# Attention features on one core: Omega loaded without its zeros, two transposes and K products moved behind a later pair's first products, half the k/q loads in another buffer ring

## The chip, the cores and the metric

The kernel runs on one core of a Trainium2 chip. The metric is the device time of one execution in microseconds (us). A core has five engines with instruction streams of their own: PE (TensorE, matrix products), DVE (VectorE), ACT (ScalarE), POOL (GpSimd) and SP (SyncE, which here only issues DMA transfers). Each stream runs in its order; where it needs another engine's result it waits on a semaphore.

## The reference

Random-feature attention, then two feed-forward layers. What the change touches is the first part, for 2 x 8 heads of 576 tokens with 64 channels and 128 features:

```python
scale = 1.0 / np.sqrt(np.sqrt(D))
q_s, k_s = (q * scale, k * scale)
def phi(x):
    proj = np.einsum('bhsd,md->bhsm', x, omega)
    h = proj - np.sum(x * x, axis=-1, keepdims=True) / 2.0
    h = h - np.max(h, axis=-1, keepdims=True)
    return np.exp(h) / np.sqrt(m)
kv = np.einsum('bhsm,bhsd->bhmd', phi(k_s), v)
z = np.sum(phi(k_s), axis=2)
out = einsum(phi(q_s), kv) / (einsum(phi(q_s), z) + 1e-06)
```

Then `x = (h * tanh(softplus(h))) @ w_out` with `h = x @ w_in` for 1152 tokens, a gate over 8 experts, and one expert of 512 x 1024 x 512 for each token. The change leaves those two layers as they are.

## The kernel before

**Pairs and steps.** Heads go in eight pairs, p = 0 to 7. A pair's tile `kqf` has the two heads' channels on 128 partitions, and its columns are groups of 128 tokens of k or q. Omega stands in a block-diagonal tile of 128 x 256 (`omf`, with `oms`, `omh`, `oml` made from it), so one product gives both heads' features. A pair is worked off in steps t = 0 to 3 (and 4, the tokens 512 to 575 of two pairs, for odd pairs), written here as (p,t). `proj(p, t)` makes a 128 x 512 result `pj`, by two times three products: L72 high part by high part, L73 high part of k/q by low part of Omega, L74 low part by high part. Only (0,0) is one plain fp32 product (L248), because it can start before k and q are split into their parts `kqh` and `kql`.

**After each step.** `phi(p, t)`: DVE takes the negated maximum (`nm`, L259), for odd t DVE also subtracts it for the q half (L264), then ACT writes exp of the k half (L266) into the tile `e`, and for even t the shifted q half as well (L269). `kvm` multiplies e of k by v into one bank, `kvp` (L278), and `qtr` transposes the q half on PE into `qt` (L299). Both are done one pair later: pair 0's at pair 1's steps.

**Result banks.** Results `pj` rotate over three banks, but some steps share a tile of two banks, `twin`:

```python
if (p, t) in ((0, 3), (1, 3)):
    st["twin"] = twin("pj")
first = {(0, 3): 0, (1, 0): 1, (1, 3): 0, (1, 4): 1}
```

So (0,3) and (1,0) lie in the two halves of one tile, and (1,3) and (1,4) in the halves of the next. The order of instructions on each engine comes from a list scheduler; `issue_after` adds a constraint to it.

**Splitting.** Pair 0 is split by ACT (L56) and DVE (L63), pair 1 by POOL (L58, L63) and partly DVE (L60), all others by POOL.

**Loads.** SP issues them all in one order, apart from Omega's (ACT, L189). All pairs' `kqf` share two buffers, `v` has three. The ring `raw` of four buffers of 128 x 512 int64 (as many bytes as 128 x 1024 fp32) takes `w_in` and `w_out` from L136.

Of the kernel before, what the change touches and what calls it, by code (L numbers as in the profile page):

```python
# [9 lines left out]
F32 = mybir.dt.float32  # L10
# [3 lines left out]
I64 = mybir.dt.int64  # L14
U32 = mybir.dt.uint32
AF = mybir.ActivationFunctionType
ALU = mybir.AluOpType
AX = mybir.AxisListType

NB, NH, SEQ, HD, M = 2, 8, 576, 64, 128  # L20
# [8 lines left out]
SCALE = 1.0 / math.sqrt(math.sqrt(HD))  # L29
# [4 lines left out]
def performer_mish_moe(  # L34
# [44 lines left out]
    ident = cs[:, 0:128]  # L79
# [51 lines left out]
    win, wo, raw = {}, {}, {}  # L131
# [53 lines left out]

    with ExitStack() as c2:
        a1 = c2.enter_context(tc.tile_pool(name="a1", bufs=1))
        omf = a1.tile([128, 2 * M], F32, name="omf")
        nc.scalar.dma_start(out=omf, in_=omt)  # L189
        omh = a1.tile([128, 2 * M], F32R, name="omh")  # L190
        oml = a1.tile([128, 2 * M], F32R, name="oml")
        a2 = c2.enter_context(tc.tile_pool(name="a2", bufs=2))
# [3 lines left out]
        wp = twin("wp")[:, 1, :]  # L196
        for _ in range(5):
            T.matmul(out=wp, lhsT=nc.const_aps.tensor(1.0, [128, 128], BF16), rhs=nc.const_aps.tensor(1.0, [128, 512], BF16), start=True, stop=True)
        oms = a1.tile([128, 2 * M], F32, name="oms")
        V.tensor_scalar(out=oms, in0=omf, scalar1=SCALE, scalar2=None, op0=ALU.mult)  # L200
        V.tensor_scalar(out=omh, in0=omf, scalar1=SCALE, scalar2=None, op0=ALU.mult)
        V.scalar_tensor_tensor(out=oml, in0=omf, scalar=SCALE, in1=omh.bitcast(F32), op0=ALU.mult, op1=ALU.subtract)
        st = {}


# [3 lines left out]
            return [slice(*c) for c in zip(cuts, cuts[1:])]  # L209

        def load(p):
            f = a3.tile([128, 1280], F32, name="kqf", tag="kqf", bufs=2)
            v = a3.tile([128, 780], F32, name="v", tag="v")
            for c in pieces(p):
                nc.sync.dma_start(out=f[:, c], in_=kq[p][:, c])
            st[p] = dict(f=f, v=v, e={})
            if p % 2 == 0:
                st[p // 2, "u"] = {}
# [18 lines left out]
        def proj(p, t):  # L237
            d = st[p]
# [4 lines that stand above are left out]
            d["p", t] = ps = st["twin"][:, first[p, t], :] if (p, t) in first else bank("pj", "pj")  # L243
            for i in range(2):
                s = slice(256 * t + 128 * i, 256 * t + 128 * i + 128)
                if (p, t) == (0, 0):

                    T.matmul(out=ps[:, i * 256 : i * 256 + 256], lhsT=d["f"][:, s], rhs=oms, start=True, stop=True)  # L248
                    continue
                with tc.issue_after(d["mm"].ins) if p == 0 and (t, i) > (1, 0) else ExitStack():  # L250
                    d["mm"] = mm3(ps[:, i * 256 : i * 256 + 256], d["h"][:, s], d["l"][:, s], omh, oml, True, True)

        def phi(p, t):

# [16 lines left out]
        def kvm(p, h):  # L271

            d, du = st[p], st[p // 2, "u"]
            if p % 2 == 0 and h == 0:
                du["K"] = bank("b0", "kvp")
            e, v, K, c = d["e"], d["v"], du["K"], (2 * h + p % 2) * 65
            for t in range(4):
                T.matmul(out=K[:, c : c + 65], lhsT=e[t][:, h, :], rhs=v[:, (2 * t + h) * 65 : (2 * t + h + 1) * 65], start=(p % 2 == 0 and h == 0 and t == 0), stop=False)  # L278
            if p % 2:
                T.matmul(out=K[:, h * 130 : h * 130 + 130], lhsT=e[4][:, h, :], rhs=v[:, 520 + h * 130 : 650 + h * 130], start=False, stop=(h == 1))  # L280

# [9 lines left out]
        def qtr(p, h):  # L291
            e, d = st[p]["e"], st[p // 2, "u"]
            if p % 2 == 0 and h == 0:
                d["qT"] = a2.tile([128, 2, 2, SEQ], F32, name="qT", tag="qT")
            qT = d["qT"]
            q = bank("qt", "qt")
            if h < 2:
                for t in range(4):
                    T.transpose(q[:, t * 128 : t * 128 + 128], e[t][:, 2 + h, :], ident)  # L299
                S.activation(out=qT[:, p % 2, h, 0:512], in_=q, func=AF.Exp)  # L300
            else:
                for i in range(2):
                    T.transpose(q[:, i * 128 : i * 128 + 128], e[4][:, 2 + i, :], ident)
                S.activation(out=qT[:, :, :, 512:SEQ], in_=q[:, 0:256].rearrange("p (h r t) -> p r h t", h=2, r=2), func=AF.Exp)
# [703 lines left out]
def _layout(a):  # L1008
    import numpy as np

    q, k, v, om = a["q"], a["k"], a["v"], a["omega"]
    kq = np.zeros((NPAIR, 128, 1280), np.float32)
    va = np.zeros((NPAIR, 128, 780), np.float32)
    for p in range(NPAIR):
        b, hp = divmod(p, NPAIR // NB)
        c = p % 2
        vm = va[p, :, 0:520].reshape(128, 4, 2, 65)
        vt = va[p - p % 2 + 1, 64 * c : 64 * c + 64, 520:780].reshape(64, 2, 2, 65)
        vm[..., 64] = 1.0
        vt[:, :, c, 64] = 1.0  # L1020
        for h in range(2):
            r = slice(64 * h, 64 * h + 64)
            for i, x in ((0, k), (1, q)):
                x = x[b, 2 * hp + h].T
                kq[p, r, 0:1024].reshape(64, 4, 2, 128)[:, :, i] = x[:, 0:512].reshape(64, 4, 128)
                kq[p - c + 1, r, 1024 + 128 * i + 64 * c : 1088 + 128 * i + 64 * c] = x[:, 512:]
            x = v[b, 2 * hp + h]
            vm[:, :, h, 0:64] = x[0:512].reshape(4, 128, 64).transpose(1, 0, 2)
            vt[:, h, c, 0:64] = x[512:]
    omt = np.zeros((128, 2, M), np.float32)  # L1030
    omt[0:64, 0] = om.T
    omt[64:128, 1] = om.T
    wi = np.ascontiguousarray(a["moe_w_in"].view(np.int64).reshape(2, 4, 2, 32, NJ, 128).transpose(4, 1, 3, 0, 2, 5)).reshape(NJ, 128, 512)
    wo = np.ascontiguousarray(a["moe_w_out"].view(np.int64).reshape(NJ, 128, 512))
    wg = np.zeros((4, 32, DM // 32, 4, E), np.float32)
    for i in range(4):
        wg[i, :, :, i] = a["moe2_w_gate"].reshape(DM // 32, 32, E).transpose(1, 0, 2)
    cst = np.zeros((128, 352), np.float32)
    cst[:, 0:128] = np.eye(128)
    cst[:, 128:224] = np.tile(np.arange(E) - 1000, NTT)  # L1040
    cst[0:TT, 224:320] = np.triu(np.ones((TT, TT)), 1)
    cst[:, 320:352] = np.tile(np.eye(32), (4, 1))
    return dict(
        kq=kq,
        va=va,
        omt=omt.reshape(128, 2 * M),
        w_in=wi,
        w_out=wo,
        wgate=wg.reshape(128, DM // 32, 32),
        w1=np.ascontiguousarray(a["moe2_w1"]),  # L1050
        w2=np.ascontiguousarray(a["moe2_w2"]),
        cap=np.asarray(a["moe2_capacity"]).astype(np.int64).reshape(1, 1),
        cst=cst,
    )
# [16 lines left out]
```

## Time and profile before

| | |
|---|---|
| median of 3 runs | 298.11 us (297.5 to 298.68) |
| the profiled execution's own time | 298.33 us |
| its span, from the first to the last instruction | 296.5 us |
| PE busy | 288.7 us, 97% of the span |
| DVE, ACT, POOL busy | 214.6, 188.1, 72.9 us |
| of the chain that ended last | PE 94%, DMA 3% |

The profile is of one execution. 1.83 us of its time lie around the span. A matmul's duration includes its pipeline, so rows overlap; the pace is read from the distance of two starts.

### The profile page before, as it was taken

How to read it: one execution, taken by the hardware profiler on the slowest of the kernel's cores; microseconds unless marked ns; L12 is line 12 of the kernel's file. 1: busy time of each engine (PE TensorE's matmuls, PEld its weight loads, DVE VectorE, ACT ScalarE, POOL GpSimd, SP SyncE). 2: the span in 40 equal slices, each digit the busy share in tenths (PEclk: the TensorE clock that was granted, in tenths of full speed). 3: DMA queues.
4: the chain of work that ended last, by engine and by line, in shares of the span. 5: the costliest groups of instructions: out<-in, count | busy, mean ns of one | idle time of the engine just before them, and what ended most of it. 6: DMA issues, size and time to landing. Idle time of an engine off the chain costs nothing.

```text
span 296.5 us, 6008 instructions
## 1 busy us (share of the span) xinstructions
PE 288.7 (97%) x2276; PEld 269.6 (91%) x2277; DVE 214.6 (72%) x394; ACT 188.1 (63%) x370; POOL 72.9 (25%) x108
## 2 busy tenths in 40 slices
PE   8999999999999999999999999999999999999992
PEld 5898888877999999999979988889999999999991
DVE  4675757996999999899897199958557674437420
ACT  4787787875194787978957989444446465245211
POOL 2798996233021101010111276200000000000000
PEclk9999999999999999999999999999999999999997
DMA  7955831221266479945610000000445528702011
GB/s 247 301 183 180 284 119 54 73 78 66 70 212 212 154 220 320 342 144 150 221 58 0 0 2 0 3 0 3 140 123 165 144 65 270 204 32 82 0 42 45
DMA packets 18433, 37.09 MB, mean 125 GB/s; under 512 B 1632, under 2 KB 7616, under 8 KB 18400
## 3 DMA queue, kind: packets, MB, share of 16 engines
q1 hardware_dynamic: 18256, 36.53, 38.8%
q8 instruction: 19, 0.31, 0.4%
q10 hardware_dynamic: 144, 0.13, 0.2%
q14 instruction: 14, 0.11, 0.2%
HBM read 33.12 MB, written 3.54 MB: 124 GB/s over the span
## 4 chain that ended last, share of the span: by engine, by line
PE 94%; DMA 3%; POOL 0%; DVE 0%; issue 0%; ACT 0%
PE h L72 12%; PE h L74 11%; PE h L73 11%; PE py L72 9%; PE py L74 9%; PE py L73 9%; PE kvp L278 4%; PE ph L74 3%; PE ph L72 3%; PE ph L73 3%; PE pj L72 3%; PE num L311 3%; PE lg L503 3%; PE pj L74 3%; PE pj L73 2%; PE qt L299 2%
## 5 line engine op out<-in xcount | busy, mean ns | idle before, releaser
L72 PE MATMUL h<-xh,wih 128*128 128x384 f32 x192 | 64.7, 337 | 0.0
L74 PE MATMUL h<-xh,wil 128*128 128x384 f32 x192 | 64.3, 335 | 0.0
L73 PE MATMUL h<-xl,wih 128*128 128x384 f32 x192 | 64.2, 334 | 0.0
L72 PE MATMUL py<-gh,whi 128*128 128x288 f32 x128 | 38.4, 300 | 0.0
L74 PE MATMUL py<-gh,wl 128*128 128x288 f32 x128 | 37.7, 295 | 0.0
L73 PE MATMUL py<-gh,whi 128*128 128x288 f32 x128 | 37.7, 294 | 0.0
L63 DVE TENSOR_TENSOR wl<-wl,whi 128x512 fp32r<-128x512 f32 x48 | 33.8, 711 | 5.3 <-PE py L74 3.6
L72 PEld LDWEIGHTS h<-xh,wih 128*128 128x128 f32 x192 | 36.0, 188 | 1.1 <-issue 1.1
L73 PEld LDWEIGHTS h<-xl,wih 128*128 128x128 f32 x192 | 36.0, 188 | 0.0
L74 PEld LDWEIGHTS h<-xh,wil 128*128 128x128 f32 x192 | 36.0, 188 | 0.0
L259 DVE TENSOR_REDUCE nm<-pj 128x4 f32<-128x512 f32 x36 | 24.3, 685 | 13.8 <-PE pj L74 13.4
L453 ACT COPY g<-h 128x384 f32<-128x384 f32 x42 | 20.0, 476 | 21.2 <-PE h L74 21.1
L58 POOL TENSOR_SCALAR wih<-wif 128x512 fp32r<-128x512 f32 x13 | 11.2, 862 | 76.8 <-PE h L73 33.0
L266 ACT ACTIVATE e<-pj,nm 128x128 f32<-128x128 f32 x72 | 22.7, 372 | 9.0 <-DVE nm L259 4.6
L497 DVE TENSOR_TENSOR g<-g,em 128x1152 f32<-128x1152 f32 x16 | 22.1, 1382 | 8.2 <-ACT em L495 8.2
L72 PEld LDWEIGHTS py<-gh,whi 128*128 128x128 f32 x128 | 24.0, 188 | 1.3 <-POOL whi L58 0.6
L73 PEld LDWEIGHTS py<-gh,whi 128*128 128x128 f32 x128 | 24.2, 189 | 0.0
L74 PEld LDWEIGHTS py<-gh,wl 128*128 128x128 f32 x128 | 24.1, 189 | 0.0
L63 DVE TENSOR_TENSOR gh<-g,gh 128x288 fp32r<-128x288 f32 x32 | 16.0, 505 | 9.9 <-ACT gh L56 9.3
L63 POOL TENSOR_TENSOR kql<-kqf,kqh 128x256 fp32r<-128x256 f32 (+1 forms) x31 | 23.0, 760 | 0.9 <-DVE kqh L60 0.6
L56 ACT CAST whi<-wl 128x512 fp32r<-128x512 f32 x39 | 23.1, 616 | 0.0
L72 PE MATMUL pj<-omh,kqh 128*128 128x256 f32 x70 | 21.7, 312 | 0.0
(151 smaller groups left out, 697.7 us busy)
## 6 DMA issues: line engine op xcount, KB each, us to landing
wi<-w_in SPq DMA_DIRECT2D x16, 512.0 KB, 3.3
wo<-w_out SPq DMA_DIRECT2D x16, 512.0 KB, 4.1
wl<-w SPq DMA_DIRECT2D x32, 256.0 KB, 3.2
kqf<-kq SPq DMA_DIRECT2D x3, 640.0 KB, 5.1
out<-zero SPq DMA_DIRECT2D x4, 448.0 KB, 6.7
v<-va SPq DMA_DIRECT2D x4, 390.0 KB, 4.7
kqf<-kq SPq DMA_DIRECT2D x3, 512.0 KB, 4.0
v<-va SPq DMA_DIRECT2D x4, 260.0 KB, 5.1
```

What stands on the lines that cost most here:

```text
L56: S.copy(out=hi, in_=src)
L58: P.tensor_scalar(out=hi, in0=src, scalar1=1.0, scalar2=0.0, op0=ALU.mult, op1=ALU.add)
L63: (P if eng == "pool" else V).tensor_tensor(out=lo, in0=src, in1=hi.bitcast(F32), op=ALU.subtract)
L72: T.matmul(out=o, lhsT=lh, rhs=rh, start=start, stop=False)
L73: T.matmul(out=o, lhsT=lh, rhs=rl, start=False, stop=False)
L74: return T.matmul(out=o, lhsT=ll, rhs=rh, start=False, stop=stop)
L259: d["max"] = V.tensor_reduce(out=nm, in_=pv, op=ALU.max, axis=AX.X, negate=True)
L266: S.activation(out=e[:, j, :], in_=pv[:, j, :], func=AF.Exp, bias=nm[:, j : j + 1])
L278: T.matmul(out=K[:, c : c + 65], lhsT=e[t][:, h, :], rhs=v[:, (2 * t + h) * 65 : (2 * t + h + 1) * 65], start=(p % 2 == 0 and h == 0 and t ...
L311: T.matmul(out=o[32 * i : 32 * i + 32, :], lhsT=d[w][:, h, r, s], rhs=d["qT"][:, r, h, t0 : t0 + n], start=True, stop=True, tile_position= ...
L453: (S.copy if 2 < j or c == 2 else V.tensor_copy)(out=g(j, slice(c * 384, c * 384 + 384)), in_=ps)
L497: V.tensor_tensor(out=hv, in0=hv, in1=em.pop(j), op=ALU.mult)
```

## The change

There are three edits.

1. **Omega.** The host sends the transposed Omega twice on top of each other (128 x 128) and not the block-diagonal 128 x 256 with zeros, so the transfer has 64 KB and not 128 KB. POOL writes the zero blocks of the three tiles. `oms` is scaled in two halves, the upper by ACT and the lower by DVE; `omh` and `oml` are made by DVE in halves, one after the other.
2. **Order.** `behind(0, 1)` makes pair 0's K products and transposes of step 1 (`e[1]`) issue after the last product of (1,0). Those of later t follow in their accumulation's order.
3. **Buffers.** The k and q of even pairs go to the ring `raw`, under the name `kqe`; odd pairs keep the two `kqf` buffers.

```diff
-        omf = a1.tile([128, 2 * M], F32, name="omf")
+        omf = a1.tile([128, M], F32, name="omf")
         nc.scalar.dma_start(out=omf, in_=omt)
...
-        V.tensor_scalar(out=oms, in0=omf, scalar1=SCALE, scalar2=None, op0=ALU.mult)
-        V.tensor_scalar(out=omh, in0=omf, scalar1=SCALE, scalar2=None, op0=ALU.mult)
-        V.scalar_tensor_tensor(out=oml, in0=omf, scalar=SCALE, in1=omh.bitcast(F32), op0=ALU.mult, op1=ALU.subtract)
+        top, low = (slice(0, 64), slice(0, M)), (slice(64, 128), slice(M, 2 * M))
+        for x in (oms, omh, oml):
+            for r, c in ((top[0], low[1]), (low[0], top[1])):
+                P.memset(x.bitcast(F32)[r, c], 0.0)
+        S.mul(out=oms[top], in_=omf[top[0], :], mul=SCALE)
+        V.tensor_scalar(out=oms[low], in0=omf[low[0], :], scalar1=SCALE, scalar2=None, op0=ALU.mult)
+        for b in (top, low):
+            V.tensor_scalar(out=omh[b], in0=omf[b[0], :], scalar1=SCALE, scalar2=None, op0=ALU.mult)
+        for b in (top, low):
+            V.scalar_tensor_tensor(out=oml[b], in0=omf[b[0], :], scalar=SCALE, in1=omh.bitcast(F32)[b], op0=ALU.mult, op1=ALU.subtract)
...
-            f = a3.tile([128, 1280], F32, name="kqf", tag="kqf", bufs=2)
+            f = a3.tile([128, 1280], F32, name="kqf", tag="kqf", bufs=2) if p % 2 else fpool.tile([128, 512], I64, name="kqe", tag="raw", bufs=4).bitcast(F32)
...
-                    d["mm"] = mm3(ps[:, i * 256 : i * 256 + 256], d["h"][:, s], d["l"][:, s], omh, oml, True, True)
+                    d["mm"] = d["mm", t] = mm3(ps[:, i * 256 : i * 256 + 256], d["h"][:, s], d["l"][:, s], omh, oml, True, True)
+
+        def behind(p, t):
+
+            return tc.issue_after(st[1]["mm", 0].ins) if (p, t) == (0, 1) else ExitStack()
...
             for t in range(4):
-                T.matmul(out=K[:, c : c + 65], lhsT=e[t][:, h, :], rhs=v[:, (2 * t + h) * 65 : (2 * t + h + 1) * 65], start=(p % 2 == 0 and h == 0 and t == 0), stop=False)
+                with behind(p, t):
+                    T.matmul(out=K[:, c : c + 65], lhsT=e[t][:, h, :], rhs=v[:, (2 * t + h) * 65 : (2 * t + h + 1) * 65], start=(p % 2 == 0 and h == 0 and t == 0), stop=False)
...
                 for t in range(4):
-                    T.transpose(q[:, t * 128 : t * 128 + 128], e[t][:, 2 + h, :], ident)
+                    with behind(p, t):
+                        T.transpose(q[:, t * 128 : t * 128 + 128], e[t][:, 2 + h, :], ident)
```

What follows is how the built programs order the instructions. Each row is one instruction, output and inputs with buffer numbers, and the semaphores that it waits on, which are named for the engine or the DMA lane that raises them.

PE before, from the end of pair 0's products on. `pj_181` is the twin of (0,3) and (1,0), `pj_229` is (1,1), `pj_244` is (1,2); `e_145`, `e_161`, `e_174` are pair 0's e of t = 0, 1, 2.

```order
L74 MATMUL pj_181<-omh_94,kql_131 128x256
L299 MATMUL qt_252<-cs_58,e_145 128x128 [waits DMAHW6_49,Activation_49]
L299 MATMUL qt_258<-cs_58,e_145 128x128 [waits Activation_49]
L299 MATMUL qt_252<-cs_58,e_161 128x128 [waits DVE_49]
L299 MATMUL qt_258<-cs_58,e_161 128x128
L278 MATMUL kvp_280<-v_116,e_145 128x65 [waits DMAHW7_49]
L278 MATMUL kvp_280<-v_116,e_161 128x65 [waits Activation_49]
L278 MATMUL kvp_280<-v_116,e_174 128x65 [waits Activation_49]
L299 MATMUL qt_252<-cs_58,e_174 128x128 [waits Activation_49]
L72 MATMUL pj_229<-omh_94,kqh_134 128x256 [waits PE_49,Pool_49]
L73 MATMUL pj_229<-oml_95,kqh_134 128x256
L72 MATMUL pj_244<-omh_94,kqh_134 128x256 [waits DVE_49,PE_49]
```

Eight more products of (1,1) and (1,2) follow, and only then the first of (1,0), `pj_181`, which waits on DVE and ACT. PE of the changed kernel from the same place; here `pj_190` is the twin, `pj_238` is (1,1), `pj_253` is (1,2), and `e_154` is pair 0's e of t = 0.

```order
L74 MATMUL pj_190<-omh_95,kql_140 128x256
L312 MATMUL qt_261<-cs_58,e_154 128x128 [waits DMAHW6_49,Activation_49]
L312 MATMUL qt_267<-cs_58,e_154 128x128 [waits Activation_49]
L290 MATMUL kvp_289<-v_125,e_154 128x65 [waits DMAHW7_49]
L72 MATMUL pj_238<-omh_95,kqh_143 128x256 [waits PE_49,Pool_49]
L73 MATMUL pj_238<-oml_96,kqh_143 128x256
L72 MATMUL pj_253<-omh_95,kqh_143 128x256 [waits DVE_49,PE_49,Activation_49]
L73 MATMUL pj_253<-oml_96,kqh_143 128x256
L74 MATMUL pj_238<-omh_95,kql_144 128x256 [waits Pool_49]
L72 MATMUL pj_190<-omh_95,kqh_143 128x256 [waits DVE_49,Activation_49]
L73 MATMUL pj_190<-oml_96,kqh_143 128x256
L74 MATMUL pj_190<-omh_95,kql_144 128x256
```

Between pair 0's last product and the first of (1,0) there are now eight instructions (two transposes, one K product, five products), and before there were nineteen (five, three, eleven). The other three transposes of pair 0's t = 1 and 2, two K products and six products come after (1,0); all six products of (1,3) then come before pair 2's first.

SP before, from the constants' load on: `kqf_126` is pair 2's, `kqf_206` pair 3's, `kqf_310` pair 4's.

```order
L347 DMA cs_58<-cst 128x352
L222 DMA v_116<-va 128x520
L222 DMA v_121<-va 128x780
L215 DMA kqf_126<-kq 128x1024
L222 DMA v_127<-va 128x520
L136 DMA wi64_412<-w_in 128x512
L215 DMA kqf_206<-kq 128x1280
L215 DMA kqf_310<-kq 128x1024
L222 DMA v_207<-va 128x780
```

SP of the changed kernel from the same place:

```order
L360 DMA cs_58<-cst 128x352
L229 DMA v_125<-va 128x520
L222 DMA kqe_135<-kq 128x1024
L229 DMA v_130<-va 128x780
L222 DMA kqf_215<-kq 128x1280
L229 DMA v_136<-va 128x520
L222 DMA kqe_319<-kq 128x1024
L222 DMA kqf_417<-kq 128x1280
L229 DMA v_216<-va 128x780
```

Pair 2's load stands before pair 1's v, pairs 3 to 5 follow at once, and the first `w_in` tile comes after all of these. Further down, the first `w_out` tile now waits on POOL (pair 6's split, whose ring buffer it takes) and stands just ahead of the v of pairs 6 and 7.

## Rows read from the trace of the kernel before

**Rows 1.** Windows: from:to, its us, each engine's busy us, PEclk, DMA share, GB/s.

```profile
5.00:10.00 5.00, 4.89 (x34) 4.29 (x34) 4.62 (x10) 3.22 (x11) 3.26 (x6) 1.00 0.99 342
10.00:15.00 5.00, 4.49 (x38) 4.29 (x37) 2.56 (x6) 3.58 (x12) 3.50 (x6) 1.00 0.85 283
15.00:75.00 60.00, 60.00 (x581) 51.32 (x580) 44.78 (x82) 44.80 (x140) 40.06 (x62) 1.00 0.39 128
```

**Rows 2.** Timeline of PE, 0 to 16 us: start, us, what, [idle before <- releaser].

```profile
0.96 2.30 PE L198 MATMUL wp<-const-bfloat16-1.0 128*128 128x512 bf16 x5 [0.96 <-PEq L1064]
...
3.73 2.07 PE L248 MATMUL pj<-oms,kqf 128*128 128x256 f32 x4 [0.46 <-DVE oms L200]
...
5.80 0.28 PE L73 MATMUL pj<-oml,kqh 128*128 128x256 f32 x1
...
7.67 0.28 PE L74 MATMUL pj<-omh,kql 128*128 128x256 f32 x1
7.79 0.62 PE L299 MATMUL qt<-cs,e 128*128 128x128 f32 x4
8.28 1.12 PE L278 MATMUL kvp<-v,e 128*128 128x65 f32 x6
...
10.95 0.34 PE L72 MATMUL pj<-omh,kqh 128*128 128x256 f32 x1
...
11.85 0.49 PE L299 MATMUL qt<-cs,e 128*128 128x128 f32 x3
12.17 1.23 PE L278 MATMUL kvp<-v,e 128*128 128x65 f32 x10
13.21 0.37 PE L72 MATMUL pj<-omh,kqh 128*128 128x256 f32 x1
...
14.20 0.39 PE L74 MATMUL pj<-omh,kql 128*128 128x256 f32 x1 [0.51 <-POOL kql L63]
```

**Rows 3.** Timeline of DVE, 3 to 10 us.

```profile
3.38 0.29 DVE L200 TENSOR_SCALAR oms<-omf 128x256 f32<-128x256 f32 x1 [2.33 <-DMA omf<-omt]
...
5.83 0.69 DVE L259 TENSOR_REDUCE nm<-pj 128x4 f32<-128x512 f32 x1 [0.34 <-PE pj L248]
...
9.72 0.41 DVE L264 TENSOR_TENSOR e<-pj,nm 128x256 f32<-128x256 f32 x1
```

**Rows 4.** Timeline of ACT, 3 to 11 us.

```profile
4.15 0.62 ACT L56 CAST kqh<-kqf 128x512 fp32r<-128x512 f32 x1 [1.67 <-DMA kqf<-kq]
5.18 0.40 ACT L56 CAST kqh<-kqf 128x256 fp32r<-128x256 f32 x1 [0.42 <-DMA kqf<-kq]
...
8.02 1.16 ACT L266 ACTIVATE e<-pj,nm 128x128 f32<-128x128 f32 x4 [0.31 <-PE pj L74]
...
10.23 0.63 ACT L266 ACTIVATE e<-pj,nm 128x128 f32<-128x128 f32 x2 [0.54 <-DVE e L264]
```

**Rows 5.** DMA issues: what, queue, count, KB each, us from issue to landing.

```profile
omf<-omt ACTq DMA_DIRECT2D x1, 128.0 KB, 2.6
```

**Rows 6.** Timeline of POOL, 12 to 41 us.

```profile
12.68 0.77 POOL L58 TENSOR_SCALAR kqh<-kqf 128x256 fp32r<-128x256 f32 x2 [1.50 <-DMA kqf<-kq]
13.42 1.42 POOL L63 TENSOR_TENSOR kql<-kqf,kqh 128x256 fp32r<-128x256 f32 x2
...
39.28 0.74 POOL L63 TENSOR_TENSOR kql<-kqf,kqh 128x256 fp32r<-128x256 f32 x1
```

**Rows 7.** Timeline of SP's DMA issues.

```profile
37.61 7.77 SPq L222 DMA_DIRECT2D v<-va  x2
```

**Rows 8.** The chain that ended last, in order of time: start, us, what.

```profile
57.35 0.84 PE kvp L278 x8
```

**Rows 9.** Windows at the end, columns as in the first group.

```profile
290.00:291.00 1.00, 0.67 (x5) 0.37 (x3) 0.13 (x1) 0.52 (x3) 0.00 (x0) 1.00 0.00 0
291.00:292.00 1.00, 0.12 (x1) 0.00 (x0) 0.50 (x2) 0.36 (x1) 0.00 (x0) 1.00 0.00 0
...
293.00:294.00 1.00, 0.00 (x0) 0.00 (x0) 0.00 (x0) 0.00 (x0) 0.00 (x0) 0.50 0.23 55
```

More of the change, by code (lines that the diff above doesn't have):

```diff
@@ L187, in performer_mish_moe @@
         a1 = c2.enter_context(tc.tile_pool(name="a1", bufs=1))
-        omf = a1.tile([128, 2 * M], F32, name="omf")
+        omf = a1.tile([128, M], F32, name="omf")
         nc.scalar.dma_start(out=omf, in_=omt)
+        oms = a1.tile([128, 2 * M], F32, name="oms")
         omh = a1.tile([128, 2 * M], F32R, name="omh")
@@ L198, in performer_mish_moe @@
             T.matmul(out=wp, lhsT=nc.const_aps.tensor(1.0, [128, 128], BF16), rhs=nc.const_aps.tensor(1.0, [128, 512], BF16), start=True, stop=True)
-        oms = a1.tile([128, 2 * M], F32, name="oms")
-        V.tensor_scalar(out=oms, in0=omf, scalar1=SCALE, scalar2=None, op0=ALU.mult)
-        V.tensor_scalar(out=omh, in0=omf, scalar1=SCALE, scalar2=None, op0=ALU.mult)
-        V.scalar_tensor_tensor(out=oml, in0=omf, scalar=SCALE, in1=omh.bitcast(F32), op0=ALU.mult, op1=ALU.subtract)
+        top, low = (slice(0, 64), slice(0, M)), (slice(64, 128), slice(M, 2 * M))
[8 more added lines that the diff above has]
+            V.scalar_tensor_tensor(out=oml[b], in0=omf[b[0], :], scalar=SCALE, in1=omh.bitcast(F32)[b], op0=ALU.mult, op1=ALU.subtract)
         st = {}
@@ L1029, in _layout @@
             vt[:, h, c, 0:64] = x[512:]
-    omt = np.zeros((128, 2, M), np.float32)
-    omt[0:64, 0] = om.T
-    omt[64:128, 1] = om.T
+    omt = np.concatenate([om.T, om.T])
     wi = np.ascontiguousarray(a["moe_w_in"].view(np.int64).reshape(2, 4, 2, 32, NJ, 128).transpose(4, 1, 3, 0, 2, 5)).reshape(NJ, 128, 512)
@@ L1045, in _layout @@
         va=va,
-        omt=omt.reshape(128, 2 * M),
+        omt=np.ascontiguousarray(omt),
         w_in=wi,
```

## The prediction, made before the changed kernel ran

> **What bounds the kernel now.** I read the windows first. From 15 to 75 us, the rest of attention, PE is busy in 60.00 of 60.00 us, so there only less PE work could save time, and the change does the same products. Between 5 and 15 us PE has holes, at a granted clock of 1.00 [rows 1]. So the change can win or lose only in the first 15 us, and what PE is late there it stays late to the end. The timeline of PE shows three holes [rows 2]. The first product, L248, starts at 3.73, when `oms` is ready. After pair 0's products (last at 7.67) PE meets transposes and K products whose operand `e` is not there yet. At (2,0), between the L72 at 13.21 and the L74 at 14.20, it waits for POOL's `kql`.
>
> Behind the second hole is a chain that PE's own speed does not shorten. DVE can take the first maximum only when L248 is done (5.83), works without a break to the subtraction of (0,3) at 9.72 [rows 3], and then ACT writes e of (0,3), 10.23 to 10.86 [rows 4]. The first product of (1,0) starts at 10.95, right behind it [rows 2]. That is the wait on ACT in the order's row of `pj_181`: (1,0) shares the twin tile with (0,3) and waits for its readers, though its half is another.
>
> **Units.** Sixteen products start between 5.80 and 7.67, so one is 0.117 us. Three transposes from 11.85 to 12.17 are 0.107 each, five K products from 12.17 to 13.21 are 0.208 each [rows 2].
>
> **Omega.** 64 KB less in the queue are at most 0.19 us at 342 GB/s [rows 1]; nothing, if the 2.6 us to landing [rows 5] are all latency. [...]
>
> Then `oms`. DVE scales all of it in 0.29 us [rows 3]. The upper half is now ACT's, and ACT needs 0.62 us for 512 columns and 0.40 for 256 [rows 4]: 0.11 for 128 columns, so 0.29 for one half of 128 x 64. So halving saves nothing, as the product waits for both halves. Bounds: if ACT takes the 0.40 of its shortest such row, 0.11 is lost; if it were as short as half of DVE's 0.29, 0.14 is won. DVE's five half operations for `oms`, `omh`, `oml` in place of three whole ones, and POOL's six memsets, are hidden: `oml` is first read by L73 at 5.80, which leaves DVE 2.4 us from 3.38 for operations on half of what took 0.29 [rows 2, 3]. Without that cover they would cost PE what they are late. I take 0.15 us won for the first product and for the whole chain behind L248; the bounds are 0.11 lost and 0.33 won.
>
> **Order.** Between 7.79 and 10.95 PE now does five transposes, three K products and eleven products. After the change only two, one and five stand ahead of (1,0), and the first of (1,0) still waits for e of (0,3). That comes 0.15 us earlier, at about 10.7, since DVE's and ACT's rows up to it are in the same order as before. The eight instructions take 2 x 0.107 + 0.208 + 5 x 0.117 = 1.01 us, and with the wait for v (its first product starts at 8.28 in before) PE is through at about 9.1. So it stands for some 1.7 us in front of an instruction that cannot start, and everything behind it in PE's order stands too, the transposes of `e[1]` and `e[2]` included, though their operands are ready. What is displaced behind the wait is 3 x 0.107 + 2 x 0.208 + 6 x 0.117 = **1.44 us**. The wait ends 0.15 us earlier: **-0.15**.
>
> One part comes back. PE's rows 13.21 to 14.20 hold two products in 0.99 us, so 0.76 us are a hole and changeover [rows 2]; `kql` of (2,0) was ready at 13.42 + 0.71 = 14.13 [rows 6]. In the changed order PE comes to (2,0) after the six products of (1,3), which before stood behind it, and three more K products: at about 10.8 + 13 x 0.117 + 6 x 0.107 + 7 x 0.208 + 6 x 0.117 = 15.1. So it finds `kql` even if POOL is no earlier: **-0.7** (0.65 to 0.76).
>
> What is late next is (1,3): it needs the twin of (0,3) and (1,0) read by ACT again. (1,0) ends six products after the restart, about 11.5; the maximum (0.69) [rows 3] and four activations (1.16) [rows 4] end it at about 13.6 with 0.25 of hand-overs. PE gets there after seven more products, six transposes and four K products, 11.5 + 0.82 + 0.64 + 0.83 = 13.8. I price it at nothing; if the hand-overs are twice that, 0.1, and at most 0.4.
>
> **Buffers.** Pair 2's load no longer waits for pair 0's buffer. POOL sat 1.50 us in front of it [rows 6], so POOL can be up to 1.5 us ahead from there on. By the line above PE no longer waits there, so I take nothing; it would be worth up to 0.76 only with the old order. On the other side v of pairs 6 and 7 now stands behind the first `w_out` tile, which waits for pair 6's split. POOL ended that by about 40 us [rows 6]; the two v were issued from 37.61 [rows 7] and first read at 57.35 [rows 8], so some 17 us hide it. Pair 1's v lands one 512 KB load later, 1.5 us at 342 GB/s, and is read only after (1,3).
>
> **Sum.** 1.44 - 0.15 - 0.7 = **+0.6 us**, bounds +0.35 to +1.3. The profiled execution took 298.33 us, so 298.9; it lies 0.22 above the median of the runs, so **298.7** against 298.11. A measurement of this kernel can tell about 0.5% (1.5 us) from no change, so this is no change.
>
> **Rivals.** *Faster: the hole does not open.* If e of (0,3) were ready when PE comes to (1,0), nothing would be displaced in vain, and PE would lose its old holes: 3.16 us between 7.79 and 10.95 less 5 x 0.107 + 3 x 0.208 + 11 x 0.117 = 2.45, so 0.7, with the 0.7 at (2,0) and the 0.15 at the start -1.55: 296.6. It decides when ACT is done by 9.1 and not 10.7. I see 0.15 of these 1.6 us; against it stands DVE, busy without a break from 5.83.
>
> *Slower: the clock falls in the hole.* At the program's end PE was busy 0.67 and 0.12 us in two windows of one us, and in the window from 293 the granted clock is 0.50, that is 1.2 GHz and not 2.4 [rows 9]. A hole of 1.7 us between busy stretches is of this kind; the longest one before, under 0.8 us, left the clock at 1.00. At the start PE ran slowly from 0.96 until about 5.80, 4.8 us [rows 2]; as long a stretch at half pace costs 2.4 us, and one as long as L248's 2.07 us costs 1.0. So 299.7 to 301.1, and it decides at whether a hole of 1.7 us is enough; the rows hold none between 0.8 us and the end's. The clock page of the Trainium skill (TensorE: Matmul & The Clock Gate, Why this matters for your kernels) warns of idle gaps between bursts for this reason; by its limit a hole as short as this one should pass, and no row here shows one.
>
> *Slower: (1,3) and what follows are late too.* ACT's four activations of (1,0) and then those of (1,1) stand between PE and each next bank; with 0.4 at (1,3) and again at (2,1) it is +1.4, 299.5.
>
> **How the numbers follow.** The forecast has 0.72, the falling clock 0.15, the late chain 0.07, no hole 0.06. Its own range is 298.0 to 299.4, from the bounds and half a microsecond of spread between runs. Stretched into the clock's case it is 297.5 to 300.6, which leaves out the fast rival and the slow end of the clock's. Faster by over 0.5%: 0.06. Slower: the clock's 0.15 and a little of the late chain, 0.17. No change: 0.77.
>
> **What would show it.** Right: PE's first L72 of (1,0) begins at about 10.8 after an idle time of some 1.7 us put down to ACT's e; no wait for `kql` at (2,0); the first product near 3.6; POOL at pair 2 by 11.5; windows from 15 us full and at 1.00. Wrong: no hole before (1,0), a granted clock under 1.00 after it, or new waits of PE for `e`, `z` or `v` from 13 to 25 us.

## The result, and the profile after

The changed kernel took **300.57 us** (median of 7 executions, 298.55 to 300.92), the kernel before on the same chip 298.15. The ratio of the executions' times is 1.0063, with a 95% interval of 1.0047 to 1.0079 (that of the two medians is 1.0081). It was run twice more below, with medians of 299.43 and 299.30 against 298.32 and 298.26, and ratios of 1.0035 (1.0021 to 1.0050) and 1.0046 (1.0023 to 1.0069). Over all 28 executions the median is 299.45. So it is about 1.1 us slower, near the half per cent (1.5 us) that a measurement of this kernel can tell, and forecast was 0.6. The 28 times lie in two groups, without which the numbers can't be understood: 19 from 298.55 to 299.87 (median 299.20), and 9 from 300.32 to 300.92, which all have a mean granted clock of 0.993 or less. Four of the first seven are of the upper group, so their median is too: it lies above the forecast's own range (298.0 to 299.4) and just inside the one that was stretched for the clock's case (up to 300.6).

The profiled execution took 298.55 us and is the shortest of its seven. Its windows, which answer to [rows 1] and [rows 9] (from:to, its us, busy us of each engine, PEclk, DMA share, GB/s):

```profile
5.00:10.00 5.00, 4.50 (x29) 3.46 (x27) 4.77 (x10) 3.29 (x12) 3.06 (x5) 1.00 1.00 365
10.00:15.00 5.00, 3.93 (x34) 3.93 (x35) 2.52 (x5) 2.74 (x9) 4.95 (x9) 1.00 1.01 413
15.00:75.00 60.00, 60.00 (x584) 51.43 (x583) 45.33 (x80) 46.01 (x143) 38.19 (x59) 1.00 0.35 117
...
291.00:292.00 1.00, 0.60 (x3) 0.37 (x3) 0.40 (x2) 0.74 (x4) 0.00 (x0) 1.00 0.00 0
292.00:293.00 1.00, 0.00 (x0) 0.00 (x0) 0.23 (x1) 0.11 (x1) 0.00 (x0) 1.00 0.00 0
...
295.00:296.00 1.00, 0.00 (x0) 0.00 (x0) 0.00 (x0) 0.00 (x0) 0.00 (x0) 0.86 0.00 0
```

PE lost busy time in the first 15 us, 0.4 and 0.6 us in the two windows, and from 15 us on nothing; the granted clock is 1.00 until the products are done. PE's timeline (start, us, what, [idle before <- releaser]), against [rows 2], shows where. Its first row is the two plain fp32 products of (0,0). Each of them is counted twice, so x4, and so is each K product; all else is counted once.

```profile
3.52 2.04 PE L255 MATMUL pj<-oms,kqe 128*128 128x256 f32 x4 [0.26 <-DVE omh L207]
...
7.80 0.28 PE L74 MATMUL pj<-omh,kql 128*128 128x256 f32 x1
8.06 0.41 PE L312 MATMUL qt<-cs,e 128*128 128x128 f32 x2
8.63 0.44 PE L290 MATMUL kvp<-v,e 128*128 128x65 f32 x2 [0.15 <-DMA v<-va]
8.87 0.36 PE L72 MATMUL pj<-omh,kqh 128*128 128x256 f32 x1
...
9.43 0.28 PE L74 MATMUL pj<-omh,kql 128*128 128x256 f32 x1
11.07 0.39 PE L72 MATMUL pj<-omh,kqh 128*128 128x256 f32 x1 [1.37 <-ACT e L277]
...
12.71 0.82 PE L312 MATMUL qt<-cs,e 128*128 128x128 f32 x6
13.36 1.00 PE L290 MATMUL kvp<-v,e 128*128 128x65 f32 x8
14.17 0.36 PE L72 MATMUL pj<-omh,kqh 128*128 128x256 f32 x1
...
15.54 0.37 PE L72 MATMUL pj<-omh,kqh 128*128 128x256 f32 x1
15.75 0.28 PE L73 MATMUL pj<-oml,kqh 128*128 128x256 f32 x1
15.87 0.28 PE L74 MATMUL pj<-omh,kql 128*128 128x256 f32 x1
...
30.55 0.69 PE L324 MATMUL den<-qT,z 128*32 128x288 f32 x8
```

The hole is there: two transposes, one K product, five products, then 1.64 us from the start at 9.43 to the one at 11.07, (1,0)'s first product. Less the 0.117 us of the product before it PE stood for 1.52 us; the row itself counts 1.37, since a duration includes the pipeline, and puts the wait down to ACT's e. At 14.17, (1,3), and at 15.54 to 15.87, (2,0), nothing is waited for: the gap at `kql` of [rows 2] is gone. The last row is the second ratio's `den`. From there on every profile here runs in step with the kernel before: PE's last transposes start 260.69 to 260.78 us behind it in all fourteen. So its start is the best mark of what PE gained or lost; in before it was at:

```profile
29.79 0.69 PE L311 MATMUL den<-qT,z 128*32 128x288 f32 x8
```

So PE was 0.76 us late, and 0.73 at its last transposes. That this execution took only 0.22 us more than the profiled one of before comes from behind PE's last row: its end, at 291.85, lies 5.0 us before the end of the span, and in before 5.4.

DVE's timeline and ACT's, against [rows 3] and [rows 4]:

```profile
5.20 0.69 DVE L63 TENSOR_TENSOR kql<-kqe,kqh 128x512 fp32r<-128x512 f32 x1 [0.80 <-ACT kqh L56]
5.81 0.68 DVE L270 TENSOR_REDUCE nm<-pj 128x4 f32<-128x512 f32 x1
...
9.89 0.41 DVE L275 TENSOR_TENSOR e<-pj,nm 128x256 f32<-128x256 f32 x1
```

```profile
4.55 0.93 ACT L56 CAST kqh<-kqe 128x512 fp32r<-128x512 f32 x2 [1.21 <-DMA kqe<-kq]
...
10.39 0.62 ACT L277 ACTIVATE e<-pj,nm 128x128 f32<-128x128 f32 x2 [0.55 <-DVE e L275]
```

The first product starts 0.21 us earlier than in before, but the first maximum only 0.02: in front of it on DVE stands the subtraction for pair 0's `kql`, which waits for ACT's cast, and that waited for pair 0's load until 4.55 (4.15 in before). A second subtraction for `kql` took 0.60 us and not the 0.41 of before. So e of (0,3) is written 0.16 us later than in before and not 0.15 earlier.

Omega's DMA issue, against [rows 5], and POOL's timeline, against [rows 6]:

```profile
omf<-omt ACTq DMA_DIRECT2D x1, 64.0 KB, 2.2
```

```profile
11.28 0.77 POOL L58 TENSOR_SCALAR kqh<-kqe 128x256 fp32r<-128x256 f32 x2
12.02 1.42 POOL L63 TENSOR_TENSOR kql<-kqe,kqh 128x256 fp32r<-128x256 f32 x2
```

Omega, now with half the bytes, landed 0.4 us sooner, and POOL is 1.40 us ahead at pair 2, as forecast (by 11.5).

### The profile page after: what moved, and what is told of

Read it like the earlier page. It is cut to its first block, busy times and chain, and to the rows that moved or that the text cites. A ratio compares the mean times of both kernels' runs of the same rounds, so it can differ in the third digit from the quotient of the medians.

```text
span 296.8 us, 6015 instructions
## 1 busy us (share of the span) xinstructions
PE 288.7 (97%) x2276; PEld 269.3 (91%) x2277; DVE 216.2 (73%) x396; ACT 188.7 (64%) x371; POOL 73.6 (25%) x114
## 4 chain that ended last, share of the span: by engine, by line
PE 94%; DVE 2%; DMA 1%; ACT 1%; issue 0%; SPq 0%; ACTq 0%
PE h L72 11%; PE h L74 11%; PE h L73 11%; PE py L72 9%; PE py L74 9%; PE py L73 9%; PE kvp L290 4%; PE pj L72 3%; PE ph L74 3%; PE ph L72 3%; PE ph L73 3%; PE num L324 3%; PE lg L516 3%; PE pj L74 3%; PE pj L73 2%; PE qt L312 2%
## 5 line engine op out<-in xcount | busy, mean ns | idle before, releaser
L56 ACT CAST gh<-g 128x288 fp32r (+1 forms) x25 | 10.8, 433 | 16.7 <-PE py L74 15.5
```

The costliest lines, as they stand in the source:

```text
L56: S.copy(out=hi, in_=src)
```

## The experiments

Twelve runs in three groups, each group on one chip with runs of before (medians 298.32, 298.26 and 298.47): in the order of the table the first four, the next four and the last four. Each has 12 executions, but `again2` 9 and `filled`, `filled8` and `deep` 6. Differences between two chips are less sure than those on one. "den" is the start of the second ratio's first `den` in each profile.

| kernel | median us | range | ratio to before, 95% | den |
|---|---|---|---|---|
| changed kernel, `again` | 299.43 | 298.62 to 300.32 | 1.0035 (1.0021 to 1.0050) | 29.74 |
| no order edit, `no_order` | 298.03 | 297.40 to 298.60 | 0.9990 (0.9976 to 1.0004) | 29.35 |
| order edit alone, `order_only` | 299.01 | 298.79 to 299.57 | 1.0031 (1.0019 to 1.0043) | 30.29 |
| hole filled, 13, `filled` | 299.83 | 299.07 to 300.30 | 1.0055 (1.0033 to 1.0076) | 30.98 |
| changed kernel, `again2` | 299.30 | 298.62 to 300.90 | 1.0046 (1.0023 to 1.0069) | 30.38 |
| no ring, `no_ring` | 299.42 | 298.88 to 300.93 | 1.0042 (1.0027 to 1.0057) | 30.54 |
| order and other banks, `own_bank` | 298.56 | 298.26 to 298.89 | 1.0006 (0.9996 to 1.0016) | 29.96 |
| other banks, no order edit, `own_bank_old` | 299.00 | 298.44 to 299.35 | 1.0020 (1.0009 to 1.0030) | 29.80 |
| deeper hole, `deep` | 300.14 | 299.82 to 301.06 | 1.0068 (1.0050 to 1.0086) | 31.34 |
| hole filled, 8, `filled8` | 299.51 | 299.13 to 300.10 | 1.0045 (1.0028 to 1.0062) | 31.01 |
| ring alone, `ring_only` | 298.50 | 297.77 to 298.92 | 1.0002 (0.9991 to 1.0013) | 29.34 |
| no order edit, cs on ACT's queue, `cs_act` | 298.79 | 298.10 to 299.54 | 1.0013 (1.0002 to 1.0025) | 31.00 |

**The parts one by one.** Without the order edit:

```
-            return tc.issue_after(st[1]["mm", 0].ins) if (p, t) == (0, 1) else ExitStack()
+            return ExitStack()
```

> The change without its order edit: Omega in halves and the ring alone. Theory A: no hole of 1.5 us, so median 297.5 to 298.3 and a spread under 1.3 us, like before. Rival C (Omega or the ring costs the time, by later loads or by more work on ACT and POOL): 299.5 to 301, as the whole change.

298.03: 1.40 us under the changed kernel on the same chip, and 0.29 under before, with an interval that holds 1. So without the order edit nothing is lost. The order edit alone is the kernel before with the function `behind` and its two uses:

> The kernel before with the order edit alone. Theory A: a hole of about 1.7 us in front of (1,0) and a median of 299.5 to 301 with a spread of 1.5 us or more. My forecast without the clock: 298.8 (0.6 over before, Omega's gain not there). Rival C: 298.1 to 298.8 with a spread under 1.3 us.

299.01, that is 0.69 over before, spread 0.78 us. The forecast's two terms for the order, 1.44 lost and 0.7 back, make 0.74. But that they agree is luck, since the hole in its profile is not the one of the changed kernel:

```profile
9.00 0.37 PE L72 MATMUL pj<-omh,kqh 128*128 128x256 f32 x1
...
10.26 0.27 PE L73 MATMUL pj<-oml,kqh 128*128 128x256 f32 x1
11.25 0.39 PE L72 MATMUL pj<-omh,kqh 128*128 128x256 f32 x1 [0.72 <-ACT e L270]
```

Here eleven products, from 9.00 to 10.26, stand ahead of (1,0) and not five. What is displaced is three transposes and two K products, 3 x 0.107 + 2 x 0.208 = 0.74 us, and with the 0.7 back nearly nothing should be left. (1,0) starts 0.30 us later than in before (11.25 and 10.95), and `den` 0.50. The ring was taken out by giving every pair its buffer in `kqf` again:

```
-            f = ... if p % 2 else fpool.tile([128, 512], I64, name="kqe", tag="raw", bufs=4).bitcast(F32)
+            f = a3.tile([128, 1280], F32, name="kqf", tag="kqf", bufs=2)
```

> The change without the ring: Omega in halves and the order alone. Forecast's sum (1.44 lost, 0.7 back at (2,0), 0.15 from Omega; the ring worth nothing): 298.7 to 299.1. Theory E (the ring costs: with it SP issues v of pair 1, pair 3, v of pair 2 and pair 4 from 4.55 to 6.28 us, so that cs and pair 0's v land later): 0.4 us or more below the changed kernel on the same chip. Rival (the ring costs nothing): within 0.25 us of it.

299.42, beside 299.30 for the changed kernel on the same chip: theory E falls, the ring costs nothing and gives nothing. It is above the 298.7 to 299.1 of the forecast's sum. PE's order is the changed kernel's, five products ahead of (1,0). As it differs from `order_only` by Omega alone, it is Omega in halves that brings the scheduler from eleven to five: six more products, 0.70 us by the units, go behind the wait. Order and Omega make +1.16 us over before and order alone +0.69, and on one chip the changed kernel is 0.42 above order alone: on top of the order edit Omega costs some 0.4 us.

That this is the price of the six products shows in a measure that leaves out when e of (0,3) comes, the distance from (1,0)'s first product to `den`. Besides the rows above and the one of `again` below, (1,0) starts in `again2` and `no_ring` at:

```profile
10.89 0.38 PE L72 MATMUL pj<-omh,kqh 128*128 128x256 f32 x1 [0.45 <-ACT e L277]
11.04 0.39 PE L72 MATMUL pj<-omh,kqh 128*128 128x256 f32 x1 [0.28 <-ACT e L277]
```

The distance is 18.84 us in before, 19.04 in `order_only`, and 19.48 to 19.50 in the three profiles of the changed kernel and in `no_ring`. So the changed order costs 0.65 us behind (1,0), where forecast was 1.44 - 0.7 = 0.74, and 0.45 of it come only with Omega in halves.

The converse edit put the ring alone into before:

> The kernel before with the ring alone. By the forecast's part on the buffers it takes PE's wait for kql at (2,0) away, which is worth up to 0.76 us with the old order: 297.5 to 298.0. Rival (the old order has other waits that end as late, so only Omega gave the 0.2 to 0.3 us of the version without the order edit): 298.1 to 298.5.

298.50 against 298.47: nothing, and the forecast's "up to 0.76 with the old order" is wrong in the time. In its profile PE has no wait for `kql` from 5 to 25 us, and `den` starts 0.45 us earlier than in before; that execution took 297.86, one of three near there, and the other nine lie from 298.25 to 298.92. What holds those up was in no profile. With 0.0 for the ring, the 0.29 us of the kernel without the order edit would be Omega's, but they are a difference between two chips and not clear of the noise.

**The shared tile.** (1,2) takes the other half of the twin tile and not (1,0):

```
-            first = {(0, 3): 0, (1, 0): 1, (1, 3): 0, (1, 4): 1}
+            first = {(0, 3): 0, (1, 2): 1, (1, 3): 0, (1, 4): 1}
```

> The changed kernel with (1,2) and not (1,0) in the other half of the twin tile, so (1,0) no longer waits for e of (0,3), which it does not read; (1,2) now does. Theory (the hole comes from that shared tile): (1,0) and (1,1), 12 products of 0.117 us, go through without a wait for ACT, what is left of the hole is under 0.9 us and stands in front of (1,2), and the median is 0.5 to 1.0 us below the changed kernel. Rival (PE has to wait for e of (0,3) anyway, whatever waits for it): within 0.25 us of it.

298.56, 0.74 us under the changed kernel, as this theory said. Four of the changed kernel's nine executions on that chip are of the upper group and none of these twelve; against the median of the other five, 299.04, it is 0.48. PE's timeline in its profile, and ACT's row of e of (0,3):

```profile
8.92 0.41 PE L312 MATMUL qt<-cs,e 128*128 128x128 f32 x2 [1.27 <-DMA cs<-cst]
9.53 0.43 PE L290 MATMUL kvp<-v,e 128*128 128x65 f32 x2 [0.20 <-DMA v<-va]
9.77 0.36 PE L72 MATMUL pj<-omh,kqh 128*128 128x256 f32 x1
...
11.15 0.28 PE L74 MATMUL pj<-omh,kql 128*128 128x256 f32 x1
11.27 0.28 PE L72 MATMUL pj<-omh,kqh 128*128 128x256 f32 x1
...
11.86 0.28 PE L74 MATMUL pj<-omh,kql 128*128 128x256 f32 x1
11.98 0.82 PE L312 MATMUL qt<-cs,e 128*128 128x128 f32 x6
```

```profile
10.10 0.63 ACT L277 ACTIVATE e<-pj,nm 128x128 f32<-128x128 f32 x2 [0.79 <-DVE e L275]
```

All 18 products go through from 9.77 to 11.98 without a wait for ACT. By the program's order the first twelve are (1,0)'s and (1,1)'s, which lie in banks of their own; they are worked off from 9.77 on, while ACT still has e of (0,3) to write (10.10 to 10.73). (1,2), which now waits for it, comes at 11.27 and finds it. `cs` came 1.27 us late here, so with the old banks the five products would have ended at 10.44 and left a wait of only some 0.4 us: the profile shows that (1,0) needs nothing of (0,3), and the times show what that is worth. So the hole was a wait for a tile whose other half (1,0) writes, and not for data: this theory holds. The 0.74 us are not the price of the tile alone, since PE's order changes with it: twelve products stand ahead of the wait, and pair 2's first two steps ahead of (1,3). The same banks in the old order:

> Omega in halves, the ring and the new banks of own_bank, without the order edit. If the shared tile also made PE wait in the old order (0.67 us of waits in front of (1,0) by before's trace): 297.3 to 297.9, up to 0.5 us below the version without the order edit, 298.03. Rival (there another wait, for kql or for cs and v, ends at the same time): 297.9 to 298.3.

299.00, a miss: about 1.0 us over the version without the order edit, on another chip. Its `den` is 0.45 us later, with gaps of 0.2 to 0.3 us behind products that start at 18.83, 20.19 and 21.19. With the new banks something waits there that did not before; for what wasn't tried.

**The clock.** The changed kernel was run again for further profiles:

> The changed kernel once more, for a second profile and more times. Theory A (the hole of 1.65 us in front of (1,0) lets TensorE's clock fall in most executions): median 299.5 to 301, spread of 1.5 us or more, and the executions with the longer span have the lower mean clock; a profile of such an execution shows a granted clock under 1.00 behind the hole, between 10 and 16 us. Rival B (the clock falls elsewhere, or only at the program's end, and the extra time is in the work itself): the same spread, but the windows from 10 to 20 us at 1.00 in every profile.

> The changed kernel a third time, on the chip of the next three kernels. So far its times lie in two clumps, near 298.8 and near 299.5 us, and now and then above 300, and the four first products took 2.04 us in one profile and 1.46 in the other, as TensorE's clock came to 2.4 GHz 0.8 us later or earlier. Theory D (that moment is what varies): the median lies between 299.0 and 300.6 with clumps about 0.8 us apart. Rival (the clock falls in the hole): the profile of an execution above 299.5 shows a granted clock under 1.00 between 10 and 20 us.

Their profiles took 298.62 and 299.20 us, both of the lower group, and the granted clock is 1.00 in every window from 0 to 290 us. In them the hole is in two parts, one in front of the first transpose, for `cs` or e (0.78 and 0.62 us), and one in front of (1,0) (0.20 and 0.45). So theory A's low clock is in no profile. What they do show is how two executions of one kernel come to differ by 0.8 us at `den`. PE's timeline of `again`, and DVE's and ACT's rows of the first maximum and of e of (0,3):

```profile
3.55 1.46 PE L255 MATMUL pj<-oms,kqe 128*128 128x256 f32 x4 [0.28 <-DVE omh L207]
...
8.38 0.41 PE L312 MATMUL qt<-cs,e 128*128 128x128 f32 x2 [0.78 <-DMA cs<-cst]
8.96 0.43 PE L290 MATMUL kvp<-v,e 128*128 128x65 f32 x2 [0.17 <-DMA v<-va]
...
10.24 0.39 PE L72 MATMUL pj<-omh,kqh 128*128 128x256 f32 x1 [0.20 <-ACT e L277]
```

```profile
5.33 0.68 DVE L270 TENSOR_REDUCE nm<-pj 128x4 f32<-128x512 f32 x1
```

```profile
9.56 0.63 ACT L277 ACTIVATE e<-pj,nm 128x128 f32<-128x128 f32 x2 [0.38 <-DVE e L275]
```

The first two products (x4) took 1.46 us and not 2.04: PE came to its full pace in the middle of them, in the first profile only behind them. The first maximum is 0.48 us earlier than in the first profile (5.33 and 5.81); there the late load held it too. On the way to e of (0,3) two operations of DVE are shorter, a subtraction for `kql` with 0.42 us and not 0.60 and a cast for pair 1 with 0.42 and not 0.58, so that e comes 0.83 us earlier (9.56 and 10.39). `den` starts at 29.74, 0.81 before the first profile's. So PE's pace, a load and DVE's durations each have a part in it.

For the upper group the hole was filled with products between the five products and (1,0). They go into one half of (1,1)'s bank, which (1,1)'s own products overwrite:

```
+FILL = 13
...
+                fill = mm3(b[:, 0:256], d["h"][:, 256:384], d["l"][:, 256:384], omh, oml, True, True)
+                for _ in range(FILL):
+                    with tc.issue_after(fill.ins):
+                        fill = T.matmul(out=b[:, 256:512], lhsT=d["h"][:, 0:128], rhs=omh, start=True, stop=True)
```

> The changed kernel with 13 more products (of 0.117 us, 1.52 us in all) that overwrite one half of the bank of (1,1), put between the five products ahead of the hole and (1,0); the output is the same. PE then works through the hole, and (1,0) still starts at about 11.1. Theory A: no fall of the clock, so median 298.3 to 299.0 and a spread under 1.3 us. Rival B or C: 300 to 301 as the changed kernel, or more.

299.83, above the 298.3 to 299.0 of theory A. The profile shows that the edit overshot, since `cs` and v came late in it (0.45 and 0.40 us) and the extra products ran on until 11.62, where e of (0,3) had been there since 11.31:

```profile
9.19 0.44 PE L300 MATMUL kvp<-v,e 128*128 128x65 f32 x2 [0.40 <-DMA v<-va]
...
10.10 1.68 PE L258 MATMUL pj<-omh,kqh 128*128 128x256 f32 x13
11.62 0.28 PE L73 MATMUL pj<-omh,kqh 128*128 128x256 f32 x1
```

So with 8 products:

> As the kernel with the filled hole, with 8 and not 13 extra products (0.94 us): with them PE stays busy until about 10.4 to 10.6 us, so that e of (0,3), ready at 10.2 to 11.0, isn't kept waiting. Clock theory: no execution of the changed kernel's high clump (above 300.2 us), and a median of 298.8 to 299.4. Rival (the high clump is not from the hole): 1 in 3 executions above 300.2.

299.51, none of six above 300.1, as the clock theory said; but with 9 in 28 that happens by chance one time in ten, and the median is again over the forecast range. In its profile `cs` came 1.35 us late and the extra products ended at 11.64, e of (0,3) at 11.01, so even eight were too many. Last the other way, a deeper hole, with (1,1)'s and (1,2)'s first products put behind (1,0)'s:

```
-                with ... else ExitStack():
+                with ... else tc.issue_after(d["mm", 0].ins) if (p, i) == (1, 0) and t in (1, 2) else ExitStack():
```

> The changed kernel with its hole made deeper: the five products of (1,1) and (1,2) that stand ahead of (1,0) go behind its first six. Of 28 executions of the changed kernel so far nine took 300.3 to 300.9 us, all nine with a mean clock of 0.993 or less; the others took up to 299.9. Clock theory (in these the clock falls in the hole, and a deeper hole lets it fall more often): more than half of the executions above 300.8, and the profile, if of one of them, shows a granted clock under 1.00 between 10 and 16 us. Rival (no fall; those executions have another cause): the five products cost 0.58 us behind the wait, so the clumps of the changed kernel moved to 299.3 to 300.5, median about 299.9, and the same share of outliers as there, at 300.9 to 301.5.

300.14, where the rival said 299.9, and one execution of six above 300.8, at 301.06. That one has a mean clock of 0.992, the other five 0.997. The clock theory wanted more than half above 300.8, and that is not so; but six executions can't tell one in six from 9 in 28. The profile (299.82 us) shows the wait and a full clock behind it, PE's timeline and the window:

```profile
11.07 0.36 PE L72 MATMUL pj<-omh,kqh 128*128 128x256 f32 x1 [1.95 <-ACT e L277]
```

```profile
10.00:15.00 5.00, 3.93 (x32) 3.74 (x33) 2.60 (x5) 2.77 (x9) 5.00 (x9) 1.00 0.99 406
```

**A version that might beat both.** The best so far, the one without the order edit, waited 1.07 us for `cs` in its profile, so `cs` went to ACT's queue:

```
         nc.scalar.dma_start(out=omf, in_=omt)
+        nc.scalar.dma_start(out=cs, in_=cst)
...
-        nc.sync.dma_start(out=cs, in_=cst)
```

> Omega in halves and the ring, no order edit, and cs issued on ACT's queue behind omf and not on SP's. PE waited 1.07 us for cs in the profile of that version; v of pair 0 goes out 0.47 us earlier too. If that wait is on the path: 297.3 to 297.8. If it is hidden by the later wait for e of (0,3): 297.9 to 298.2.

298.79, a miss: 0.76 us over the version without this edit (on another chip; 0.61 when each is set against before on its own), where 0.2 to 0.7 less were expected. ACT's timeline and PE's:

```profile
5.21 0.93 ACT L56 CAST kqh<-kqe 128x512 fp32r<-128x512 f32 x2 [1.81 <-DMA kqe<-kq]
```

```profile
5.93 0.55 PE L72 MATMUL pj<-omh,kqh 128*128 128x256 f32 x1 [0.31 <-issue]
...
8.91 0.41 PE L72 MATMUL pj<-omh,kqh 128*128 128x256 f32 x1
9.12 0.41 PE L73 MATMUL pj<-oml,kqh 128*128 128x256 f32 x1
...
10.15 0.38 PE L313 MATMUL qt<-cs,e 128*128 128x128 f32 x2
```

Pair 0's k and q, which the first cast waits for and which now go out beside `cs`, come at 5.21 (4.06 in the profile without this edit), and in this execution PE ran pair 0's products at 0.21 us each, about half its pace, until 10 us. Which of the two costs the time was not separated. So no version here is measurably better than before: the one without the order edit is the best, at 0.9990 with an interval that holds 1.

## Why the prediction was right, and where it was not

**The hole: right in place, near in size.** Forecast was (1,0)'s start at 10.7 to 10.8 with PE standing for some 1.7 us, put down to ACT's e. It was 11.07 after 1.52 us (1.37 by the row). The cause, the shared tile, is shown by `own_bank`, where no product waits for ACT and 0.74 us come back. But the size belongs to that execution: in `again`, `again2` and `no_ring` PE first waited for `cs` or e in front of the transposes, and the wait at (1,0) was 0.20 to 0.45.

**The sum on PE: right.** Forecast +0.6. PE was +0.76 late at `den` in the first profile and +0.59 in the third; in the second, where e of (0,3) came 0.83 us earlier, -0.05. Two of its three terms, 1.44 lost and 0.7 back, are borne out behind (1,0): 0.65 and not 0.74, in all three. The third, e 0.15 us earlier, depends on the execution: (1,0) started 0.12 later than in before's profile, 0.71 earlier and 0.06 earlier. That order alone measured 0.69 beside 0.74 says nothing for the sum, since it has eleven products ahead of the wait.

**Omega: the step that did not hold.** I took "0.15 us won for the first product and for the whole chain behind L248". The transfer saved more than my bound of 0.19: DVE starts on Omega at 3.04 and not 3.38. Of these 0.34 us the first product got 0.21; its row puts the end of its wait down to `omh`, which stands behind `oms` on DVE. The chain did not follow. In the first profile DVE's first maximum stands behind the subtraction for `kql`, and that behind a load; I had read DVE as bound by PE's first product alone [rows 3]. In `again2` and `no_ring` that load was in time and the first maximum was 0.25 and 0.18 us earlier than in before (5.58 and 5.65), but the gain went on a later load (pair 0's second part, pair 1's), and e of (0,3) came at 10.21 and 10.36 beside 10.23. And I had costed the two edits apart: in the old order Omega wins at most about 0.3 us, with the order edit it costs about 0.4, since it brings the scheduler to put six more products behind the wait. I had counted with the right five, so the sum was not hurt by it.

**`kql` at (2,0): right, but for what the ring is worth.** The wait is gone, as forecast, and for the reason forecast, that PE comes there later: it is gone without the ring too, in `no_ring` and `order_only`. It is also gone with the ring alone, and there the time did not move (298.50 against 298.47). I had said that the ring would be worth up to 0.76 us in the old order.

**(1,3), buffers and the two v: right.** No wait of PE for e at 14.17, the ring worth nothing beside the order edit (299.42 and 299.30), and windows from 15 us on full.

**The clock in the hole: open, with much for it.** The difference between the lower group (+0.9 us over before's 298.3) and the median of the first seven (+2.4) is the upper group: that this median is near my range's end is four of seven falling there, 9 of 28 in all. Of the 46 executions of kernels that have five products or fewer ahead of an unfilled hole (the changed kernel, `no_ring`, `deep`), 12 lie 1 us or more above the median of the rest of their kernel, all with a mean clock of 0.993 or less; of the 72 of the other kernels with no such hole none does. The 12 of the two filled kernels are left out; one, at 300.30 with 0.993, could be either. Two of the twelve have 0.987, that is 299 x 0.013 x 2 = 7.8 us at the lower level, and behind PE's last row there are only 5.0 to 5.8 us of span in the three profiles of the changed kernel; so in those two the clock was also low while PE still worked. Over the groups the mean clock is 0.9914 in the upper and 0.9959 in the lower, an estimated 0.0045 x 299 = 1.3 us of full clock lost, and the upper group is 1.5 us longer: about what a low clock costs where PE is busy. This price lies in my rival's 1.0 to 2.4, and its share, 9 of 28, above my 0.15. But by the means alone it can't be told where the clock was low, in the hole or before PE's last products: 0.993 occurs in the lower group too, since the fall at the end comes sooner or later (in before's profile within the window from 292, in the changed kernel's within the one from 295). The deeper hole did not make such executions more frequent in six, and no profile caught one. So the hole as their cause is argued and not shown. On the page that I cited (the Trainium skill, TensorE: Matmul & The Clock Gate, Why this matters for your kernels): the profiled holes, up to the wait of 1.95 us in `deep`, left the clock at 1.00, with products of 0.117 us behind them, which agrees with its limit; whether the executions at 0.987 do is open.

## What to carry to other kernels

Before an instruction is moved ahead, list every wait it carries, the tile's too: a product that writes one half of a shared tile waits for the readers of the other half, and whatever is put behind it waits with it. Where a scheduler makes the order, edits don't add: two that win or lose alone can bring another order together, so each pair has to be laid side by side on the engine that bounds. And where an effect is as small as the spread, take a mark on the bounding engine behind the changed stage (here the second `den`), or the distance of two marks, which leaves out what varies ahead of both, several profiles of one kernel, and look whether the times fall into groups before trusting a median of seven.

## What the runs showed of the hardware that was not expected

PE's full pace comes at a moment that differs between executions of nearly the same start. The first two products (x4) took 1.43 to 2.08 us in the profiles here, and PE came to its full pace within them in `again`, at 7.5 us in `ring_only` and at 10 in `cs_act`. The windows' granted clock says 1.00 there too, so at the start the pace has to be read from the spacing of the products. In `again` the early pace is part of what brought `den` 0.81 us forward; in `ring_only`, with the old order, PE at half pace until 7.5 us still came to `den` at 29.34, as early as any.

`cs`, issued at 3.13 or 3.14 us in every profile where SP issues it, made PE wait nothing in before and 0.27 to 1.35 us in eight of the others, with and without the ring. And DVE's cast of 128x256 for pair 1, which stands in front of the maximum of (0,3), took 0.28 us in before and in the changed kernel's first profile, 0.60 in `order_only`, 0.68 in `no_order` and 0.81 in `filled`; why was not tried.
